# A clustered attention with an MLP: a step of the weights' narrowing on GpSimd, and other places for the first turned probabilities and the second queries

## The chip, the cores and the metric

One core of a Trainium2 chip (trn2) runs the whole program. Times are device microseconds. TensorE does the matmuls, VectorE, ScalarE and GpSimd the elementwise work, SyncE issues the DMAs.

## The reference

`q`, `k`, `v` have the shape (4, 8, 768, 64) in f32. Queries and keys are each given to one of 16 clusters of their head, and a query attends only to keys of its own cluster. The result, 3072 tokens x 512, goes through an MLP whose weights arrive in f64.

```python
q_assign = argmax(q_n @ c_n.T); k_assign = argmax(k_n @ c_n.T)       # normed
mask = q_assign[:, :, :, None] == k_assign[:, :, None, :]
scores = where(mask, scale * q @ k.T, -1e9)
attn = exp(scores - max); attn = attn / (sum(attn) + 1e-9)
x = (attn @ v), heads side by side                                    # 3072 x 512
h = x @ w_in                                                          # 512 x 2048
g = s * relu(h) ** 2 + b
out = g @ w_out                                                       # 2048 x 512
```

## The kernel before

**Units.** The attention is cut into 192 units: batch, chunk of 256 queries, pair of heads, half chunk, head. A unit is 128 queries against 768 keys. `scores` makes its 128x768 scores in PSUM from f16 halves, the cluster mask folded in; `maxima` takes the row maxima on VectorE (L533); `exps` has ScalarE make the bias (L540) and the probabilities `p` (L543), f32.

**The first 16 units** (`TURN`, `RAW`) turn `p` on TensorE (L567) into PSUM; VectorE and ScalarE copy one half each to `PT` (L142, L141), and `values` multiplies `PT` in f32 with the raw values (L591). From unit 16 on `p` is split into two f16 halves (`high`, `low`), turned by a DMA, and `value` multiplies them with the value halves `vh`, `vl` (L626 to L628). Those halves are made by `prep_v` (L491, L223, L225) in the tile `halves`, five places of one head pair each.

**Weights.** `weights` loads w_in and w_out in 32 pieces, 128x512 f64 each, as pairs of 32-bit words into stages: three buffers of the tag "stage", a part of `keys`, and `gs`. `rebase` (L246, ScalarE) turns the high word into an f32 whose exponent is moved, `narrow` (L250, L251, VectorE) shifts it up by three bits and puts the three top bits of the low word below. `bound` (L256 to L264) takes the sums and the maxima. Two pieces are asked for in every step of the main loop. A stage is loaded again (L92) once its piece is narrowed. When all are narrowed, `wsplit` (L309, L312) scales each piece and splits it into f16 halves.

**The MLP** follows 21 units behind (`LAG`): `mlp_in` (L684), `mlp_relu` (L691 to L694), `mlp_gl` (L699, GpSimd), `mlp_out` (L711), a step for each of 16 column blocks of each chunk. Its x tiles come from `finish_x` (L648, L651) into `xs_kept`, nine places. Until they are needed, three places at a time hold `kb` of the first batch's head pairs 1 to 3 (L353).

**Queries.** `prep_q` is a generator that the loop takes one yield further in each step: load, maximum over the chunk (L409, L412), scale (L415 to L418), split into `qb`, `qa` (L223, L225), copy (L429), DMA transposes into `QA`, `QB` (L433, L446), with the cluster mask between (L445). Chunk 0's two parts are made before the loop, chunk 1's begin at steps 6 and 14.

**Order.** The program is written once, unrolled, and a planner with its own times orders each engine's instructions by program order and readiness; units before 20 are asked for with priority (`first_of_all`), and some helpers are tied behind an instruction (`behind`). Each engine then takes its queue in order. Tiles of one tag share their places: `p`, `ph`, `PT`, `ka`, `qa`, `qb` and three of the first query loads have the tag "big", with 11 places (`BIGN`) of 3 KB a partition.

Of the kernel before, what the change touches and what calls it, by code (L numbers as in the profile page):

```python
# [8 lines left out]
F16 = mybir.dt.float16  # L9
BF16 = mybir.dt.bfloat16  # L10
F32 = mybir.dt.float32
I32 = mybir.dt.int32
U32 = mybir.dt.uint32
AF = mybir.ActivationFunctionType
ALU = mybir.AluOpType
# [3 lines left out]
P = 128  # L19
C = 16  # L20
D = 64
# [5 lines left out]
def tile_cluster_attention_mlp(ctx, tc, q, k, v, cent, w_in, w_out, s_in, b_in, out):  # L27
    nc = tc.nc
    B, H, S, _ = q.shape
    NT, DM = out.shape  # L30
    DFF = w_in.shape[1]
    T = S // P
    NP = H // 2
    CT = 2
# [5 lines left out]
    V = nc.vector  # L40
    G = nc.gpsimd
    A = nc.scalar
    LAG = 21
    BIGN = 11

    RAW = 16
# [5 lines left out]
    sb = ctx.enter_context(tc.tile_pool(name="sb", bufs=2))  # L52
# [5 lines left out]
    def const(shape, dt, name):  # L58
        return cp.tile(shape, dt, tag=name, name=name)
# [5 lines left out]
    def inverse2(eng, dst, src, e):  # L65
        eng.tensor_scalar(dst.bitcast(I32), src.bitcast(I32), -1, (254 + e) << 23, op0=ALU.mult, op1=ALU.add)

    def scale2(dst, src):
        bits = dst.bitcast(I32)
        V.tensor_scalar(bits, src.bitcast(I32), EXPMASK, None, op0=ALU.bitwise_and)  # L70
        V.tensor_scalar(bits, bits, -1, 253 << 23, op0=ALU.mult, op1=ALU.add)
        V.tensor_scalar(dst, dst, 2.0 ** 60, None, op0=ALU.min)
# [14 lines left out]
    def load(dst, src, free=False):  # L87
        if last_transpose[0] is None or free:
            nc.sync.dma_start(dst, src)
        else:  # L90
            with tc.issue_after(last_transpose[0].ins):
                nc.sync.dma_start(dst, src)  # L92
# [4 lines left out]
    def columns(n, name):  # L97
        return sb.tile([P, n], BF16, tag=f"amb{n}", name=f"amb_{name}", bufs=3)
# [10 lines left out]
    def allmax(dst, src, name, bank="m"):  # L109
        n = src.shape[1]  # L110
        if bank == "turned":
            pm = turned[:, 0]
        else:
            pm = small_bank(f"am_{name}", bank)
        for j in range(n):
            nc.tensor.matmul(pm[:, j * P : (j + 1) * P], src[:, j : j + 1].broadcast_to([P, P]), identb, start=True, stop=True)
        V.tensor_reduce(dst, pm[:, : n * P].rearrange("p (n q) -> p n q", q=P), axis=AX.X, op=ALU.max)

    def absmax(dst, src, axis=AX.X):
        return V.tensor_reduce(dst, src, axis=axis, op=ALU.max, apply_absolute_value=True)  # L120
# [69 lines left out]
    xs_kept = const([P, 9, CT, 2, P], F16, "xk")  # L190
# [4 lines left out]
    halves = const([P, 5, VHW + VLW], F16, "halves")  # L195
# [20 lines left out]
    def split(hi, lo, src, f, early):  # L216
        if early:
            A.activation(src, src, AF.Copy, scale=f)
            last_split[1] = A.activation(hi, src, AF.Copy)
            yield  # L220
            G.tensor_tensor(lo, src, hi, op=ALU.subtract)
        else:
            last_split[1] = A.activation(hi, src, AF.Copy, scale=f)  # L223
            yield
            last_split[0] = V.scalar_tensor_tensor(lo, src, f, hi, op0=ALU.mult, op1=ALU.subtract)  # L225
# [18 lines left out]
    def rebase(d):  # L244
        hw = d["st"][:, :, :, 1].bitcast(F32)
        A.activation(d["w"], hw, AF.Prelu, scale=2.0 ** -112, alpha=-(2.0 ** 32))  # L246

    def narrow(d):
        c = d["w"].bitcast(I32)
        V.tensor_scalar(c, c, 3, None, op0=ALU.logical_shift_left)  # L250
        V.scalar_tensor_tensor(c.bitcast(U32), d["st"][:, :, :, 0].bitcast(U32), 29, c.bitcast(U32),  # L251
                               op0=ALU.logical_shift_right, op1=ALU.bitwise_or)

    def bound(d):
        w, p, ft = d["w"], d["p"], d["ft"]
# [138 lines left out]
    def prep_q(b, c, hq):  # L394
        n = f"{b}_{c}_{hq}"
        nh = 4
        if b or c > 1 or c + hq > 1:
            qn = sb.tile([P, CT * DM], F32, tag="stage", name=f"qn_{n}", bufs=3)
        else:
            qn = sb.tile([P, T * P], F32, tag="big", name=f"qn_{n}", bufs=BIGN)  # L400
        qn = qn[:, : nh * CT * D].rearrange("p (h t d) -> p h t d", h=nh, t=CT)
        load(
            qn, q[b, nh * hq : nh * hq + nh].rearrange("h (p t) d -> p h t d", t=T)[:, :, c * CT : (c + 1) * CT, :]
        )
        yield
        prs = slice(2 * hq, 2 * hq + 2)
        sm = sb.tile([P, 4, 2], F32, tag="qsm", name=f"qsm_{n}", bufs=3)
        qm = columns(2, f"q{n}")
        absmax(qm, qn.rearrange("p (j h) t d -> p j (h t d)", j=2))  # L409
        if b + c:  # L410
            yield
        allmax(sm[:, 1, :], qm, f"q{n}", "m" if b or c > 1 else "h")  # L412
        yield
        f = sm[:, 2, :]
        scale2(f, sm[:, 1, :])  # L415
        V.tensor_tensor(f, f, KSM[b][:, 3, prs], op=ALU.min)
        V.tensor_tensor(sm[:, 1, :], f, KSM[b][:, 2, prs], op=ALU.mult)
        inverse2(V, sm[:, 3, :], sm[:, 1, :], -3)  # L418
        qa = sb.tile([P, 2 * T * P], F16, tag="big", name=f"qa_{n}", bufs=BIGN)[:, : nh * CT * 2 * D].rearrange("p (h t e d) -> p h t e d", h=nh, t=CT, e=2)
        qb = sb.tile([P, 2 * T * P], F16, tag="big", name=f"qb_{n}", bufs=BIGN)[:, : nh * CT * 2 * D].rearrange("p (h t e d) -> p h t e d", h=nh, t=CT, e=2)  # L420
        both = []
        for j in range(2):
            hs = slice(2 * j, 2 * j + 2)
            both.append(split(qb[:, hs, :, 0, :], qa[:, hs, :, 0, :], qn[:, hs], sm[:, 2, j : j + 1], b + c == 0))
        for z in zip(*both):
            yield
        for z in both:
            next(z, None)
        G.tensor_copy(qa[:, :, :, 1, :], qb[:, :, :, 0, :])  # L429
        QA = sb.tile([P, nh * CT, P], F16, tag="QA", name=f"QA_{n}", bufs=2)  # L430
        QB = sb.tile([P, nh * CT, P], F16, tag="QB", name=f"QB_{n}", bufs=2)
        QS[(b, c, hq)] = (QA, QB, sm)
        last_qa[0] = nc.sync.dma_start_transpose(QA, qa.rearrange("p h t e d -> p (h t e d)"))  # L433
        yield
        yield
        pa = small_bank(f"pq_{n}", "m" if b or c > 1 else "h")
        for h in range(nh):
            hc = slice((nh * hq + h) * C, (nh * hq + h + 1) * C)
            for t in range(CT):
                i = h * CT + t  # L440
                o = pa[:, i * C : (i + 1) * C]
                nc.tensor.matmul(o, QA[:, i, :], cT[:, 0, hc], start=True, stop=False)
                nc.tensor.matmul(o, QA[:, i, :], cT[:, 2, hc], start=False, stop=True)
        mk = qb.rearrange("p h t e (r c) -> p (h t) e r c", c=C)[:, :, 1, :, :]
        yield from onehot(pa, nh * CT, f"q{n}", mk, BIG, 0.0, G if b or c or hq else V)  # L445
        last_qb[0] = nc.sync.dma_start_transpose(QB, qb.rearrange("p h t e d -> p (h t e d)"))  # L446
# [108 lines left out]
    def low(i):  # L555
        u = U[i]
        if i < TURN:
            n = T // 2
            flat = sb.tile([P, T * P], F32, tag="big", name=f"PT_{i}", bufs=BIGN) if i < RAW else None
            two = None if i < RAW else sb.tile([P, 2, T * P], F16, tag="big", name=f"PT_{i}", bufs=BIGN)  # L560
            if i < RAW:
                u["PT"] = flat.rearrange("p (n q) -> p n q", n=T)
            else:
                u["PT"] = two.rearrange("p e (n q) -> p (e n) q", q=P)
            for e in range(2):
                for kt in range(n):
                    nc.tensor.transpose(turned[:, e, kt * P : (kt + 1) * P], u["p"][:, (e * n + kt) * P : (e * n + kt + 1) * P], ident)  # L567
                cols = slice(e * n * P, (e + 1) * n * P)
                if i < RAW:
                    done = copy((V, A)[e], flat[:, cols], turned[:, e, : n * P])  # L570
                    if i == RAW - 1:
                        last_copy[e] = done
                else:
                    A.activation(two[:, 0, cols], turned[:, e, : n * P], AF.Copy)
                    V.tensor_tensor(two[:, 1, cols], turned[:, e, : n * P], two[:, 0, cols], op=ALU.subtract)
            return
        G.tensor_tensor(u["ph"][:, 1, :], u["p"], u["ph"][:, 0, :], op=ALU.subtract)  # L577
        u["PT"] = sb.tile([P, 2 * T, P], F16, tag="big", name=f"PT_{i}", bufs=BIGN)
        last_transpose[0] = nc.sync.dma_start_transpose(u["PT"], u["ph"].rearrange("p e s -> p (e s)"))  # L579
# [229 lines left out]
    i = 0  # L809
    while i < NU + 8 or i - LAG < NS + 4:  # L810
# [28 lines left out]
        if 0 <= i - 1 < NU:  # L839
            with first_of_all(i):  # L840
                low(i - 1)
# [38 lines left out]
```

## Time and profile before

| | |
|---|---|
| median of 3 runs | 907.15 us (906.84 to 907.77) |
| profiled execution | 905.56 us, span 903.9 us |
| TensorE busy | 823.4 us (91%) |
| ScalarE busy | 710.7 us (79%) |
| VectorE busy | 636.9 us (70%) |
| GpSimd busy | 548.2 us (61%) |
| TensorE's mean granted clock | 0.971 |

Busy times are sums over the span, and instructions of one engine can overlap by some 0.1 us. The profile has views by stretch, by line, by tile, of waits, of the chain that ended last, and of the instructions in order of time. PE is TensorE, PEld its weight load, DVE VectorE, ACT ScalarE, POOL GpSimd, SPq SyncE's queue of DMAs. L12 is line 12 of the kernel.

### The profile page before, as it was taken

What the parts mean: (1) busy time and instruction counts of PE and PEld (TensorE: products, weight loads), DVE (VectorE), ACT (ScalarE), POOL (GpSimd) and SP (SyncE); (2) the same over time, 40 slices, a digit from 0 to 9 for tenths busy, and PEclk for the clock granted to TensorE, in tenths of its full rate; (3) what the DMA queues carried; (4) which work ended last, traced back from release to release, by engine and by line L of the source; (5) the groups of instructions that cost most, each with busy time, mean ns of one, the idle gap of its engine ahead of it and who ended that gap; (6) DMA issues with size and microseconds to landing.
All of it is one profiled execution on the core that took longest, in us unless ns stands there. A gap on an engine that the chain in (4) does not pass through costs nothing.

```text
span 903.9 us, 22830 instructions
## 1 busy us (share of the span) xinstructions
PE 823.4 (91%) x8625; PEld 584.7 (65%) x8625; DVE 636.9 (70%) x1673; ACT 710.7 (79%) x1406; POOL 548.2 (61%) x580
## 2 busy tenths in 40 slices
PE   1575869878999999999999999999999999999997
PEld 0464646545677767777766767777677777677764
DVE  8798898998778678658877667669777667563200
ACT  4578868875788879888888788987889888888553
POOL 3110147666587668768777677777876667576321
PEclk9996788997999999999999999999999999999999
DMA  5999536766797998979899879689997687676200
GB/s 154 214 334 305 158 71 147 163 138 137 159 184 151 193 199 144 180 146 187 173 168 205 192 150 181 165 142 198 188 158 166 129 138 162 121 157 122 59 25 23
DMA packets 437758, 144.23 MB, mean 160 GB/s; under 512 B 405392, under 2 KB 434064, under 8 KB 437648
## 3 DMA queue, kind: packets, MB, share of 16 engines
q1 hardware_dynamic: 437648, 142.78, 75.3%
q8 instruction: 67, 1.10, 0.6%
q14 instruction: 43, 0.35, 0.1%
HBM read 35.69 MB, written 6.29 MB: 46 GB/s over the span
## 4 chain that ended last, share of the span: by engine, by line
PE 51%; DVE 19%; DMA 12%; ACT 8%; issue 5%; POOL 2%; SPq 2%; DVEq 0%; ACTq 0%; POOLq 0%
PE h L684 18%; PE acc L711 16%; PE sc L523 8%; DVE ssm L533 3%; DMA kn<-in_k_dram 3%; DMA qn<-in_q_dram 2%; PE sc L626 2%; PE sc L628 2%; PE sc L627 2%; ACT p L543 2%; DVE ka L225 2%; DVE wis L312 1%; DMA vn<-in_v_dram 1%; ACT ssm L540 1%; SPq L579 1%
## 5 line engine op out<-in xcount | busy, mean ns | idle before, releaser
L577 POOL TENSOR_TENSOR ph<-p,ph 128x768 f16<-128x768 f32 x176 | 297.5, 1690 | 145.2 <-ACT ph L141 48.0
L684 PE MATMUL h<-xk,wis 128*128 128x256 f16 x2304 | 290.1, 276 | 10.6 <-DVE wis L312 3.3
L711 PE MATMUL acc<-wos,gs 128*128 128x512 f16 x1152 | 280.0, 379 | 2.2 <-DVE o L719 0.9
L684 PEld LDWEIGHTS <-wis 128*128 128x128 f16 x2304 | 223.6, 99 | 70.0 <-issue 4.1
L543 ACT ACTIVATE p<-sc,ssm,qsm 128x768 f32<-128x768 f32 x192 | 189.5, 987 | 4.1
L533 DVE TENSOR_REDUCE ssm<-sc 128x1 f32<-128x768 f32 x192 | 181.8, 948 | 3.2 <-PE sc L523 3.1
L699 POOL TENSOR_TENSOR gs<-r,gs 128x256 f16<-128x256 f32 x192 | 139.0, 725 | 67.2 <-ACT r L694 57.2
L711 PEld LDWEIGHTS <-gs 128*128 128x128 f16 x1152 | 104.0, 98 | 95.9 <-ACT gs L693 1.3
L540 ACT ACTIVATE ssm<-ssm,lift,qsm 128x1 f32<-128x1 f32 x192 | 73.5, 383 | 91.7 <-DVE ssm L533 91.3
L141 ACT ACTIVATE ph<-p 128x768 f16<-128x768 f32 x164 | 137.5, 838 | 0.5
L691 ACT ACTIVATE r<-h,cf 128x256 f32<-128x256 f32 x192 | 89.2, 465 | 37.6 <-PE h L684 30.8
L626 PE MATMUL sc<-halves,PT 128*128 128x65 f16 x1032 | 113.3, 196 | 0.3 <-DMA PT<-ph 0.3
L627 PE MATMUL sc<-halves,PT 128*128 128x64 f16 x1032 | 113.1, 193 | 0.0
L628 PE MATMUL sc<-halves,PT 128*128 128x65 f16 x1032 | 112.8, 193 | 0.0
L626 PEld LDWEIGHTS <-PT 128*128 128x128 f16 x1056 | 99.2, 98 | 12.1 <-DMA PT<-ph 0.9
L627 PEld LDWEIGHTS <-PT 128*128 128x128 f16 x1056 | 98.3, 99 | 11.7 <-issue 0.8
L523 PE MATMUL sc<-keys,QA 128*128 128x384 f16 x384 | 98.4, 338 | 7.9 <-ACT p L543 5.9
L523 PE MATMUL sc<-keys,QB 128*128 128x384 f16 x384 | 99.1, 339 | 6.0 <-DMA QB<-qb 5.9
L628 PEld LDWEIGHTS <-PT 128*128 128x128 f16 x1056 | 98.4, 98 | 0.0
L632 DVE TENSOR_SCALAR ssm<-sc 128x1 f32<-128x1 f32 x172 | 26.3, 153 | 82.4 <-PE sc L628 80.8
L694 ACT ACTIVATE r<-r 128x256 f32<-128x256 f32 x192 | 79.4, 415 | 3.8
L693 ACT ACTIVATE gs<-r 128x256 f16<-128x256 f32 x192 | 78.9, 412 | 1.3
(191 smaller groups left out, 1097.6 us busy)
## 6 DMA issues: line engine op xcount, KB each, us to landing
kn<-in_k_dram SPq DMA_DIRECT2D x16, 384.0 KB, 3.9
qn<-in_q_dram SPq DMA_DIRECT2D x24, 256.0 KB, 3.4
vn<-in_v_dram SPq DMA_DIRECT2D x16, 384.0 KB, 4.1
out_dram<-o SPq DMA_DIRECT2D x12, 512.0 KB, 3.4
wst<-in_moe_w_in_dram SPq DMA_DIRECT2D x10, 512.0 KB, 5.6
wst<-in_moe_w_out_dram SPq DMA_DIRECT2D x10, 512.0 KB, 5.7
PT<-ph SPq DMA_TRANSPOSE x176, 3.5
gs<-in_moe_w_out_dram SPq DMA_DIRECT2D x3, 512.0 KB, 4.4
```

The source lines that it names most:

```text
L141: return A.activation(dst, src, AF.Copy)
L523: last_score[0] = nc.tensor.matmul(sc[:, e, :HALF], X[:, col, :], y[:, h * S + e * HALF : h * S + (e + 1) * HALF], start=st, stop=not st)
L533: last_max[0] = V.tensor_reduce(SM[i // 4][:, 0, j : j + 1], U[i]["sc"], axis=AX.XY, op=ALU.max, negate=True)
L543: last_exp[0] = A.activation(p.rearrange("p (a b) -> p a b", a=2), u["sc"], AF.Exp, bias=bi, scale=u["scale"], **total)
L577: G.tensor_tensor(u["ph"][:, 1, :], u["p"], u["ph"][:, 0, :], op=ALU.subtract)
L626: nc.tensor.matmul(o1, PT[:, kt, :], vh[:, h, kt, : D + 1], start=(kt == 0), stop=False)
L627: nc.tensor.matmul(o, PT[:, kt, :], vl[:, h, kt, :], start=False, stop=False)
L628: nc.tensor.matmul(o1, PT[:, T + kt, :], vh[:, h, kt, : D + 1], start=False, stop=(kt == T - 1))
L684: nc.tensor.matmul(ph[:, :CW], WSP[ft][0][:, wl, kt, :], XS[(b, c, kt)][:, :, xl, :], start=(i == 0), stop=(i == len(terms) - 1))
L691: last_relu[0] = A.activation(r, ph[:, :CW], AF.Relu, scale=MS[(b, c)][0])
L699: G.tensor_tensor(g[:, 1, :], r, g[:, 0, :], op=ALU.subtract)
L711: nc.tensor.matmul(acc[:, t, :], g[:, gl, rows], WSP[ft][1][:, wl, :], start=(ft == 0 and gl + wl == 0), stop=(ft == NF - 1 and gl == 1))
```

## The change

Three edits. In `rebase` GpSimd turns the low word, in place in the stage, into its three top bits: as a number it is multiplied by 0.9375 / 2^29, 0.03125 is taken off, and the conversion to an integer gives 0 to 7. `narrow` is then one instruction, a shift by three and an or. In `prep_q` the tiles `qa`, `qb` of batch 0, chunk 1 (both parts) lie in places 4 to 7 of `xs_kept` and not in the tag "big". In `low` the turned probabilities of the first 16 units lie in places 0 to 3 of `halves`, by the unit's number modulo 4, and not in the tag "big".

```diff
     def rebase(d):
         hw = d["st"][:, :, :, 1].bitcast(F32)
         A.activation(d["w"], hw, AF.Prelu, scale=2.0 ** -112, alpha=-(2.0 ** 32))
+        lw = d["st"][:, :, :, 0]
+        G.tensor_scalar(lw, lw.bitcast(U32), 0.9375 * 2.0 ** -29, -0.03125, op0=ALU.mult, op1=ALU.add)
 
     def narrow(d):
         c = d["w"].bitcast(I32)
-        V.tensor_scalar(c, c, 3, None, op0=ALU.logical_shift_left)
-        V.scalar_tensor_tensor(c.bitcast(U32), d["st"][:, :, :, 0].bitcast(U32), 29, c.bitcast(U32),
-                               op0=ALU.logical_shift_right, op1=ALU.bitwise_or)
+        V.scalar_tensor_tensor(c.bitcast(U32), c.bitcast(U32), 3, d["st"][:, :, :, 0].bitcast(U32),
+                               op0=ALU.logical_shift_left, op1=ALU.bitwise_or)
...
-        qa = sb.tile([P, 2 * T * P], F16, tag="big", name=f"qa_{n}", bufs=BIGN)[:, : nh * CT * 2 * D].rearrange("p (h t e d) -> p h t e d", h=nh, t=CT, e=2)
-        qb = sb.tile([P, 2 * T * P], F16, tag="big", name=f"qb_{n}", bufs=BIGN)[:, : nh * CT * 2 * D].rearrange("p (h t e d) -> p h t e d", h=nh, t=CT, e=2)
+        if b == 0 and c == 1:
+            qa, qb = (xs_kept[:, j : j + 2].rearrange("p n t e q -> p (n t e q)") for j in (4, 6))
+        else:
+            qa, qb = (sb.tile([P, 2 * T * P], F16, tag="big", name=f"q{'ab'[j]}_{n}", bufs=BIGN) for j in range(2))
+        qa, qb = (z[:, : nh * CT * 2 * D].rearrange("p (h t e d) -> p h t e d", h=nh, t=CT, e=2) for z in (qa, qb))
...
-            flat = sb.tile([P, T * P], F32, tag="big", name=f"PT_{i}", bufs=BIGN) if i < RAW else None
+            flat = halves[:, i % 4, : 2 * T * P].bitcast(F32) if i < RAW else None
```

## Rows read from the trace of the kernel before

**Rows 1.** Busy us and instructions by stretch, granted clock, DMA share, GB/s.
```profile
25.00:110.00 85.00, 58.45 (x463) 46.45 (x463) 73.07 (x183) 64.72 (x144) 8.33 (x11) 0.84 0.92 257
110.00:130.00 20.00, 15.82 (x133) 11.83 (x132) 18.45 (x52) 15.61 (x28) 10.30 (x9) 0.91 0.25 54
130.00:220.00 90.00, 71.67 (x711) 48.24 (x712) 83.27 (x184) 66.16 (x127) 56.65 (x50) 0.89 0.62 141
220.00:400.00 180.00, 179.41 (x1980) 126.12 (x1978) 131.50 (x348) 150.13 (x291) 128.35 (x129) 1.00 0.90 174
```

**Rows 2.** SyncE's waits to 220 us: total, times, longest.
```profile
SPq L92 <- DVE wo L251: 12.0, 9, 2.1
...
SPq L92 <- DVE wi L251: 10.0, 7, 3.0
```

**Rows 3.** VectorE in order of time: start, us, line.
```profile
122.84 0.28 DVE L611 TENSOR_TENSOR xs<-px,ssm 128x128 f32<-128x128 f32 x1
```

**Rows 4.** The chain that ended last: start, us, what.
```profile
136.04 2.74 PE h L684 x12
```

**Rows 5.** The narrowing by line: busy us, mean ns of one.
```profile
L250 DVE TENSOR_SCALAR wi<-wi 128x512 int32<-128x512 int32 x15 | 6.3, 421 | 2.3 <-ACT wi L246 2.1
L250 DVE TENSOR_SCALAR wo<-wo 128x512 int32<-128x512 int32 x15 | 6.3, 418 | 1.2 <-ACT wo L246 1.2
L251 DVE SCALAR_TENSOR_TENSOR wi<-wst,wi 128x512 uint32<-128x512 uint32 x9 | 6.1, 682 | 0.0
```

**Rows 6.** GpSimd's groups by line, over the span.
```profile
L429 POOL COPY qa<-qb 128x512 f16<-128x512 f16 x24 | 17.9, 747 | 3.3 <-ACT qb L223 3.3
...
L337 POOL TENSOR_SCALAR qb<-oo_q 128x512 f16<-128x512 f16 x23 | 14.3, 624 | 15.4 <-DVE oo_q L336 8.2 <-DVE ssm L632 4.5 <-DVE ssm L633 1.2
...
L337 POOL TENSOR_SCALAR kb<-oo_k 128x768 f16<-128x768 f16 x12 | 10.0, 830 | 1.2 <-DVE oo_k L336 0.6 <-DMA qn<-in_q_dram 0.3 <-PE h L684 0.3
...
L376 POOL COPY xk<-ka 128x768 f16<-128x768 f16 x3 | 3.8, 1294 | 0.0
...
L142 POOL CAST ph<-p 128x768 f16<-128x768 f32 x3 | 2.5, 824 | 4.3 <-issue 4.3
```

**Rows 7.** One meeting of VectorE and GpSimd, in order of time.
```profile
88.47 1.17 DVE L251 SCALAR_TENSOR_TENSOR wi<-keys,wi 128x512 uint32<-128x512 uint32 x1
...
88.42 0.67 POOL L651 TENSOR_TENSOR xn<-xs,xn 128x256 f16<-128x256 f32 x1 [4.48 <-ACT xn L648]
```

**Rows 8.** Around the second queries, ScalarE and VectorE in order of time.
```profile
74.64 0.38 ACT L540 ACTIVATE ssm<-ssm,lift,qsm 128x1 f32<-128x1 f32 x1
...
90.47 0.49 ACT L223 ACTIVATE qb<-qn,qsm 128x256 f16<-128x256 f32 x1
90.86 0.97 ACT L543 ACTIVATE p<-sc,ssm,qsm 128x768 f32<-128x768 f32 x1
...
85.75 0.42 DVE L117 TENSOR_REDUCE qsm<-am_q 128x2 f32<-128x256 f32 x1
...
90.23 0.55 DVE L142 COPY PT<-turned 128x384 f32<-128x384 f32 x1
```

**Rows 9.** Busy by stretch, as in rows 1.
```profile
60.00:70.00 10.00, 6.47 (x59) 5.16 (x56) 10.00 (x26) 7.21 (x16) 2.44 (x3) 1.00 1.08 364
70.00:90.00 20.00, 11.33 (x68) 8.96 (x68) 17.68 (x49) 16.72 (x39) 1.49 (x2) 0.65 1.03 301
```

**Rows 10.** Around the value halves: instructions in time, and a tile's products.
```profile
113.77 0.78 PE L591 MATMUL px<-vn,PT 128*128 128x64 f32 x6
...
114.58 0.93 ACT L223 ACTIVATE halves<-vn,vm 128x768 f16<-128x768 f32 x1
...
L626 PE MATMUL sc<-halves,PT x120: 192/194/262, 126.3 to 228.1; 128*128 128x65 f16 x120
```

**Rows 11.** GpSimd's waits to 115 us: total, times, longest.
```profile
POOL xn L651 <- ACT xn L648: 23.0, 3, 14.9
POOL oe_k L334 <- DVE ssm L608: 21.9, 2, 19.6
```

## The prediction

> **What bounds the kernel now.** I read the busy times by stretch first. From 220 us on TensorE is busy 179.41 of 180 us to 400 [rows 1], and the slices of the page stay at nine tenths or more to the end: that part is TensorE's own work, and nothing in the change alters a matmul. The open time lies ahead of it: TensorE idles 26.6 us in 25 to 110, 4.2 in 110 to 130 and 18.3 in 130 to 220, 49 us in all. The engine that is full there is VectorE: 73.07 of 85, 18.45 of 20, 83.27 of 90 us (86%, 92%, 93%) [rows 1]. ScalarE has 64.72 of 85 and GpSimd only 8.33 of 85, so in the first stretch GpSimd is free for 76.7 us. The DMA engines show a share of 0.92 at 257 GB/s there.
>
> The first stretch is the loading of the 32 weight pieces (4 KB a partition). SyncE's waits show that the loads are held back by the narrowing: 12.0 and 10.0 us behind L251 [rows 2]. It closes where the first MLP step opens: the last xs product of the first x chunk comes at 122.84 [rows 3], the second step's matmuls of h run from 136.04 [rows 4]. Both inputs, weights and first 16 units, come through VectorE. What VectorE saves before 123 us therefore moves the whole TensorE-bound rest forward, until another resource is as full.
>
> **The change part by part.**
>
> *The shift that goes.* L250 is one instruction for each of 32 pieces, 15 + 15 of them at 421 and 418 ns in the rows, two more on pieces that lie in other tiles: 32 x 0.42 = 13.4 us of VectorE [rows 5], all while weights load. L251 stays one instruction with two SBUF operands of the same shapes; only its two operations change, and I keep its 682 ns.
>
> *The new GpSimd step.* 32 instructions of 128x512, one 32-bit operand with a step of two words, converted twice. No row shows this. Nearest below: the GpSimd scalar operation 128x512 in f16, 624 ns; in 128x768 32-bit words are no dearer than 16-bit ones (cast from f32 824, scalar operation in f16 830). Nearest above: the copies of 128x768 into xk at 1294 [rows 6]. I take 0.75, the mean of the 128x512 copies (747): 32 x 0.75 = 24 us, inside 76.7 us of idle GpSimd; at 1.29 it is 41 us and still fits. It runs beside ScalarE's L246 and waits for the same landing, so the narrowing starts when the later of the two is done. Queued behind it on GpSimd stand the first batch's cluster masks (L334, L337) and the xn differences (L651): each comes at most one step, 0.75 us, later.
>
> On the price, the Trainium skill (GPSIMD Engine Reference, section "Performance pitfalls for Q7 kernels") has a rule against this step: reads at a stride above 8 bytes cost about 2.9 cycles an element in place of 1.9. The step here is just 8 bytes, and no row here has it. By the page's 1.2 GHz the estimate would be 0.81 us on the near side and 1.24 on the far, and the gain summed up below would be smaller by 0.6 us, or by 5 us.
>
> *What it costs VectorE.* The two engines get in each other's way: L251 takes 0.68 us [rows 5], but 1.17 us at 88.47, when GpSimd's xn ran from 88.42 to 89.09 [rows 7]: 0.49 lost to an overlap of 0.62. With GpSimd's new step filling 24 of 85 us, 28% of the 32 L251 meet one, and lose half of 0.75: 32 x 0.28 x 0.375 = 3.4 us. Bounds: 0 (the planner sets them apart) and 32 x 0.49 = 15.7 (each meets one). Left on VectorE: 13.4 - 3.4 = 10.0 us. The row of VectorE's load says how much of that can be time: 86% of 10.0 = 8.6 us.
>
> *The places of the tag "big".* Probabilities p, their transposes PT, ka, qa and qb share 11 places. In the rows the exponentials wait for this tag: the bias of one unit was ready at 74.64 + 0.38, its scores stood in PSUM, ScalarE was working on weights, and yet its p came at 90.86. In the same half microsecond came the first write into qb (90.47) and into the next PT (90.23) [rows 8]. Three tiles of one tag starting together after 15 us says that the places are given out in program order and that qb, whose scale waits for the maximum L117 at 85.75, stood at the head. In the change neither qa, qb of these two chunks nor the 16 PT are asked of this tag, so p no longer queues behind them. What is that worth? VectorE was 89% busy in the gap, with weights [rows 9]: the exponentials move forward and weights back. Only the idle VectorE time can be won, 85 - 73.07 = 11.9 us in the stretch at most, nothing at least. I take 1 us, since the row for 70 to 90 has 2.3 us idle.
>
> *The new places' own waits.* PT of unit i lies where that of unit i-4 was, and needs values(i-4) done, one step earlier in program order: 0. The value halves of head pair 0 can now be written only after values(12). ScalarE writes them at 114.58 today; the last products of that call ran at 113.77 + 0.78 = 114.55 [rows 10], so nothing moves by more than it does already. If the planner were to put the two further apart, the first product that reads the halves is at 126.3 [rows 10], 10 us behind 114.58 + 0.93, with VectorE's half of the split between; ahead of that cover it costs nothing, beyond it every microsecond is one. The four memsets of the halves' last columns (L491), which wait for nothing today, now wait for values(12) and values(14) in GpSimd's queue, and the differences of p wait behind them: I charge 0.5 us, between 0 and 5. qa and qb of the two second chunks lie in kept tiles; the second pair comes eight steps after the first, and the key copies that lay there belong to steps up to 3: 0.
>
> **The sum.** 8.6 + 1.0 - 0.5 = 9.1 us. The profiled execution took 905.56 (span 903.9 and 1.66 around it), so 896.5; the median of the runs, 907.15, stands 1.59 above it, so 898.0.
>
> **The rivals.**
>
> *The loads pace it (0.15).* If the DMA's share of 0.92 is the limit, only the loop through a stage buffer shortens. 85 us for 32 pieces are 2.66 a piece, five stages make a loop of 13.3 us; 0.42 less in it is 3.2% of 85, 2.7 us: about 904.5. For it: the share. Against: 364 GB/s were reached in 60 to 70 beside 301 in 70 to 90 [rows 9], so the 21.8 MB of the stretch would need 60 us and not 85, and SyncE waited for L251.
>
> *Moving work between these two engines wins nothing (0.12).* At 1.29 us a step GpSimd fills 41 of 85 us, 48% of the L251 meet one and lose 0.65: 10 us of the 13.4, and 86% of 3.4 is 2.9, less the 0.5 of the places and with nothing from the gap, 2.4 at the best; and with each narrowing started late behind the longer step it is under the 1.8 us that can be told: 905.5 to 908. The Trainium skill (Perfetto Trace Analysis, section "Optimizing Scalar/DVE Operations") says as much: the two share a read port, so offloading from one to the other might not help. The trace agrees in kind (0.68 to 1.17 us); in size it has one such case in 32 pieces, since GpSimd is nearly idle.
>
> *Slower: the weights fall into GpSimd's queue (0.13).* GpSimd takes its instructions in order, and in this stretch it stands long behind others: 23.0 us in xn for ScalarE and 21.9 in oe_k for VectorE [rows 11]. Today that costs nothing. Put a weight step behind such a one and the narrowing waits, and VectorE behind it, and the next load. It decides from 9.1 us passed on, 20% of the 44.9; at a third it is 15 us, and the run ends at 907 + 6 = 913. Against: GpSimd issues of this kind are few (some 11 in 85 us), and the order written down follows when operands come.
>
> *More than that (0.13).* If the freed exponentials also close most of VectorE's 11.9 us of idle, the gain is near 10.0 + 6 = 16: 891.
>
> **How the numbers follow.** My forecast (893 to 902.5 is its own range) has 0.47. A measurement of this kernel tells 0.2%, 1.8 us, from no change. Faster: 0.47 + 0.13 + 0.15 = 0.75; same 0.12; slower 0.13. The range 888 to 909 leaves out about 0.04 below and 0.13 above; it holds the loads' rival, the rival without gain and the contention's and the gap's bounds but for their ends.
>
> **What would show it.** L250 gone and L251 still near 0.68 us, its mean under 0.8; a GpSimd group on the weight stages, 32 times, 0.6 to 0.9 us; the last narrowing some 7 us earlier; p within 2 us of its bias near unit 10; the second step's h 6 to 10 us before 136; TensorE's idle time to 220 near 41 us; the stretch behind it unchanged. I am wrong if VectorE shows waits for the GpSimd step beyond some 5 us, if that step takes over 1.3 us, if SyncE's waits for L251 vanish and the last load comes no earlier, or if value products wait for the halves.

## The result and the profile after

The changed kernel takes 917.23 us (median of 4 runs, 912.79 to 918.39) beside 907.0 of the kernel before (906.67 to 907.77): ratio 1.0103, 95% interval 1.0066 to 1.0139. By the ratio it is slower by about 9.3 us (10.2 between the two medians), where 9.1 us less was forecast. Its profiled execution took 916.1 us with a span of 914.4.

The lines of the changed kernel stand one lower from the weights on (narrowing L252, GpSimd's step L248), four lower from the scores on (p L547, h L688, relu L695, acc L715).

First the busy times by stretch, as in rows 1, and two stretches of the TensorE-bound part on their own.

```profile
25.00:110.00 85.00, 61.74 (x467) 49.45 (x468) 69.80 (x155) 66.28 (x147) 31.16 (x46) 0.83 0.93 260
110.00:130.00 20.00, 15.09 (x143) 12.21 (x143) 18.04 (x49) 15.45 (x27) 10.38 (x12) 0.86 0.32 67
130.00:220.00 90.00, 71.30 (x727) 47.80 (x727) 83.38 (x189) 66.09 (x127) 58.37 (x50) 0.92 0.68 140
220.00:400.00 180.00, 173.92 (x1909) 122.40 (x1906) 127.51 (x327) 148.19 (x286) 127.23 (x128) 1.00 0.86 168
...
325.00:420.00 95.00, 87.59 (x974) 62.67 (x973) 62.77 (x176) 76.35 (x152) 63.94 (x65) 1.00 0.82 154
420.00:560.00 140.00, 134.52 (x1527) 95.36 (x1525) 102.44 (x274) 115.11 (x224) 101.30 (x103) 1.00 0.86 173
```

The same two stretches in the kernel before:

```profile
325.00:420.00 95.00, 94.93 (x1072) 67.91 (x1070) 67.59 (x195) 83.23 (x163) 71.17 (x69) 1.00 0.89 166
420.00:560.00 140.00, 136.46 (x1535) 97.17 (x1534) 103.19 (x272) 116.20 (x228) 101.81 (x105) 1.00 0.89 177
```

From 25 to 220 us TensorE's work is about what it was: 148.1 us against 145.9 [rows 1]. The time is lost where nothing was edited. From 220 us to the end of the span, the changed kernel first, TensorE works as long as before and idles 22.7 us where it idled 10.9:

```profile
220.00:914.40 694.40, 671.73 (x7244) 475.00 (x7240) 443.73 (x1182) 554.59 (x1090) 463.04 (x470) 1.00 0.76 150
```
```profile
220.00:903.85 683.85, 672.94 (x7272) 475.51 (x7269) 441.23 (x1186) 554.14 (x1091) 461.92 (x470) 1.00 0.78 152
```

Most of that is one stretch: from 325 to 420 TensorE idled 0.07 us before and idles 7.41 now, at full clock in both. TensorE's waits from 220 to 620 us (what waited, for whom: us in total, times, longest), the changed kernel first, then the kernel before:

```profile
PE h L688 <- ACT r L695: 3.0, 2, 2.4
PE pk L389 <- DMA keys<-ka: 2.5, 1, 2.5
PE sc L527 <- ACT p L547: 2.2, 2, 1.3
PE am_q L116 <- DVE ssm L636: 1.9, 2, 1.1
PE acc L715 <- DVE o L723: 1.3, 1, 1.3
PE h L688 <- DMA xk<-xn: 1.1, 1, 1.1
```

```profile
PE sc L523 <- DMA QB<-qb: 1.9, 2, 1.3
PE acc L711 <- DVE o L719: 0.6, 1, 0.6
PE am_q L116 <- DVE ssm L632: 0.6, 1, 0.6
```

Many small waits of different kinds have come: for an MLP step's relu, for a key transpose of the third batch, for scores in PSUM whose probabilities are not yet made. Another order of the same instructions could look like that, and the programs bear it out: behind the first 44 units no instruction differs, yet 2070 of TensorE's 6947 from there on, 288 of VectorE's 1129 and 280 of ScalarE's 1043 stand in another place of their engine's queue. The planner has redone the rest from a slightly different start; why its new order is the worse one is not shown. Counted by relu instructions of the MLP, the changed kernel is 2.4 us ahead at the 41st, 4.4 behind at the 49th, 10.0 behind at the 97th and 10.5 at the last.

The edits themselves did what they say. The groups of GpSimd's step and of the narrowing to 110 us (busy us, mean ns of one | idle before):

```profile
L248 POOL TENSOR_SCALAR wst<-wst 128x512 int32<-128x512 uint32 x20 | 14.3, 717 | 25.3 <-DMA wst<-in_moe_w_in_dram 10.8 <-DVE ssm L609 6.0 <-DMA wst<-in_moe_w_out_dram 5.1
...
L252 DVE SCALAR_TENSOR_TENSOR wo<-wo,wst 128x512 uint32<-128x512 uint32 x9 | 7.0, 782 | 0.0
L252 DVE SCALAR_TENSOR_TENSOR wi<-wi,wst 128x512 uint32<-128x512 uint32 x9 | 6.6, 734 | 1.2 <-POOL wst L248 1.2
L252 DVE SCALAR_TENSOR_TENSOR wi<-wi,gs 128x512 uint32<-128x512 uint32 x3 | 3.0, 1002 | 0.0
...
L252 DVE SCALAR_TENSOR_TENSOR wo<-wo,gs 128x512 uint32<-128x512 uint32 x3 | 2.1, 688 | 1.1 <-POOL gs L248 1.1
```

And the eleventh unit's bias and probabilities, those of rows 8, on ScalarE; then the last narrowing, on VectorE, and the second MLP step's matmuls of h (start, us):

```profile
76.09 0.38 ACT L544 ACTIVATE ssm<-ssm,lift,qsm 128x1 f32<-128x1 f32 x1
...
78.34 0.97 ACT L547 ACTIVATE p<-sc,ssm,qsm 128x768 f32<-128x768 f32 x1
```

```profile
108.34 0.67 DVE L252 SCALAR_TENSOR_TENSOR halves<-halves,wst 128x512 uint32<-128x512 uint32 x1
```
```profile
132.89 2.74 PE L688 MATMUL h<-xk,wis 128*128 128x256 f16 x12 [1.89 <-DVE oe_q L333]
```

The wait of 16 us ahead of p [rows 8] is now 1.9. But the last weight is narrowed at 108.34, where it was at 103.85 before. The second step's h comes some 3 us ahead of the 136.04 of [rows 4].

### The profile page after: what moved, and what is told of

It reads as the page before. It is cut to its first block, busy times and chain, and to the rows that moved or that the text cites. A ratio compares the mean times of both kernels' runs of the same rounds, so it can differ in the third digit from the quotient of the medians.

```text
span 914.4 us, 22839 instructions
## 1 busy us (share of the span) xinstructions
PE 824.4 (90%) x8625; PEld 587.1 (64%) x8625; DVE 635.1 (69%) x1641; ACT 711.8 (78%) x1406; POOL 573.2 (63%) x612
## 5 line engine op out<-in xcount | busy, mean ns | idle before, releaser
L688 PE MATMUL h<-xk,wis 128*128 128x256 f16 x2304 | 289.1, 275 | 14.2 <-DVE oe_q L333 3.7
L715 PE MATMUL acc<-wos,gs 128*128 128x512 f16 x1152 | 285.3, 380 | 5.4 <-POOL gs L703 3.8
L688 PEld LDWEIGHTS <-wis 128*128 128x128 f16 x2304 | 223.8, 99 | 73.5 <-issue 10.1
L547 ACT ACTIVATE p<-sc,ssm,qsm 128x768 f32<-128x768 f32 x192 | 189.2, 985 | 4.0
L715 PEld LDWEIGHTS <-gs 128*128 128x128 f16 x1152 | 104.1, 98 | 96.5 <-POOL gs L703 5.2
L695 ACT ACTIVATE r<-h,cf 128x256 f32<-128x256 f32 x192 | 89.1, 465 | 46.3 <-PE h L688 37.7
```

Source lines behind the costliest of these rows:

```text
L547: last_exp[0] = A.activation(p.rearrange("p (a b) -> p a b", a=2), u["sc"], AF.Exp, bias=bi, scale=u["scale"], **total)
L688: nc.tensor.matmul(ph[:, :CW], WSP[ft][0][:, wl, kt, :], XS[(b, c, kt)][:, :, xl, :], start=(i == 0), stop=(i == len(terms) - 1))
L695: last_relu[0] = A.activation(r, ph[:, :CW], AF.Relu, scale=MS[(b, c)][0])
L715: nc.tensor.matmul(acc[:, t, :], g[:, gl, rows], WSP[ft][1][:, wl, :], start=(ft == 0 and gl + wl == 0), stop=(ft == NF - 1 and gl == 1))
```

## The experiments

Three theories. *Order*: the loss comes from the planner's new order of the untouched rest. *Edits*: one of the edits costs more than it saves. *Loads*: the saved VectorE time was worth less than I said, since the DMA engines pace the start too. To part them, kernels can hold each engine's queue to a recorded order by ties without semaphores between neighbours; the table of positions is left out here:

```diff
+    traced = nc.cur_bb.bb.instructions[cut:]      # cut: 0 (wholeorder) or where step 44 begins (oldtail, newtail)
+    for name, code in ORDER.items():              # per engine: the recorded order
...
+        for first, then in zip(line, line[1:]):
+            tc.add_manual_dep(then, first.name, DependencyInfo(NoSync, DATA), reason="order")
```

Each kernel was timed beside runs of the kernel before on the same chip (907.5 to 907.7 us in each set). One kernel's runs spread over 5 to 10 us, so the ratio with its interval is what counts. A difference worked out from two such ratios is less sure than either.

**The rest's order, both ways.** `changed_oldtail` is the whole change with the order of before from step 44 on; `before_newtail` is the kernel before with the changed kernel's order there.

> The changed kernel, all its work kept; what is traced from step 44 on (some 250 us into the run) is held, engine by engine, to the order that the kernel before has there. Theory 1 (the loss is the planner's new order of that part, whose instructions the change does not touch): the start's gain of 2 to 3 us stays and the loss of 13 us goes, 904 to 905.5 us. Rival (the new GpSimd step or the new places cost it, by what they do): as slow as the changed kernel, 913 to 918.

> The kernel before, none of the change; from step 44 on held to the changed kernel's order. Theory 1: the 13 us of loss appear without the change, 917 to 921 us. Rival: no edit, no loss, 906 to 908.

Measured: 907.86 us, ratio 1.0000 (0.9984 to 1.0017), and 915.16 us, 1.009 (1.0065 to 1.0115). Without any edit the new order alone costs some 8 us; without it the whole change costs nothing. Both sizes are under theory 1's forecast: the lead of 2 to 3 us that the start showed in the profile is not there in the time. TensorE's clock is no rival: its mean was 0.971 to 0.978 in the changed kernel's runs and 0.970 in those of the kernel before. The trace of `before_newtail` shows the same hole at the same place, and the same waits. The two stretches as above, then TensorE's waits from 220 to 620 us (its lines stand 31 lower than before's):

```profile
325.00:420.00 95.00, 87.63 (x973) 62.48 (x972) 63.93 (x176) 76.52 (x153) 64.11 (x64) 1.00 0.81 155
420.00:560.00 140.00, 135.38 (x1547) 96.11 (x1544) 102.99 (x277) 116.20 (x227) 101.50 (x104) 1.00 0.86 175
```

```profile
PE h L715 <- ACT r L722: 2.8, 2, 2.3
PE pk L419 <- DMA keys<-ka: 2.2, 1, 2.2
PE sc L554 <- ACT p L574: 1.7, 4, 0.8
```

**One edit at a time, the rest as before.** `bits_oldtail` has GpSimd's step and the shorter narrowing alone, `places_oldtail` both new places without them (the hunks of the change's diff that belong to each), each with the old order from step 44 on and the planner's own order ahead of it.

> Only the GpSimd step of the weights, the rest as before; from step 44 on in the order of the kernel before, so that the time shows the start alone. If the saved shift is worth what the prediction said, 898 to 900 (8.6 us). If the loads or the other queues take it back, 904 to 907. If GpSimd's queue delays the start, over 908.

> Only the new places (turned probabilities, second queries), the weights as before; from step 44 on in the order of the kernel before. If closing the gap before the eleventh exponential only swaps work on VectorE, 906 to 907 (the prediction gave it 1 us). If it is what gains the 2 to 3 us of the start, 904 to 905. Over 908 if the new places make waits of their own.

Measured: 903.55 us, 0.9956 (0.9934 to 0.9978), and 911.71 us, 1.0032 (1.0016 to 1.0047). The weights' step wins about 4 us, the places lose about 3, together nothing.

**Is the bad order tied to one edit?** `bits_ownorder` is the weights' step alone, with whatever order the planner gives.

```diff
-        V.tensor_scalar(c, c, 3, None, op0=ALU.logical_shift_left)
-        V.scalar_tensor_tensor(c.bitcast(U32), d["st"][:, :, :, 0].bitcast(U32), 29, c.bitcast(U32), ...)
+        V.scalar_tensor_tensor(c.bitcast(U32), c.bitcast(U32), 3, d["st"][:, :, :, 0].bitcast(U32), ...)
+        G.tensor_scalar(lw, lw.bitcast(U32), 0.9375 * 2.0 ** -29, -0.03125, op0=ALU.mult, op1=ALU.add)
```

> The kernel before with the GpSimd step and the shortened VectorE step alone, in the order that the planner itself gives (no order held). Theory 'order' (the ten us come from the way in which the planner reorders the untouched work from step 44 on; this kernel gets the same order there as the changed kernel but for some 200 places on TensorE's list): the 903.6 of the same edit with the order of before held there, plus 7.5 to 9.5: 911 to 913. Theory 'the places alone bring the bad order': 903 to 905.

Measured: 913.92 us, 1.0064 (1.004 to 1.0088). The best of the edits, alone, falls into nearly the same order (some 200 of TensorE's places differ from the changed kernel's) and loses 10 us by it.

**Why the weights' step is worth 4 us and not 8.6.** Five kernels in the order of before over the whole run, with only what is added to them placed freely. `bits_wholeorder` is the weights' step. The others take the kernel before and change one load: `noshift_wholeorder` leaves the shift out with no GpSimd step in its place (its weights then have other values), `extra_gpsimd_wholeorder` adds GpSimd's step and keeps both VectorE instructions, `two_shifts_wholeorder` shifts twice, and `more_dma_wholeorder` adds transfers that nothing waits for:

```diff
# noshift
-        V.tensor_scalar(c, c, 3, None, op0=ALU.logical_shift_left)
# extra_gpsimd
+        G.tensor_scalar(lw, lw.bitcast(U32), 0.9375 * 2.0 ** -29, -0.03125, ...)
# two_shifts
         V.tensor_scalar(c, c, 3, None, op0=ALU.logical_shift_left)
+        V.tensor_scalar(c, c, 0, None, op0=ALU.logical_shift_left)
# more_dma
         load(st.rearrange("p a f w -> p a (f w)"), src)
+        if p % 2 == 0:
+            nc.sync.dma_start(unread[p // 2], w_out.bitcast(I32)[ft * P : (ft + 1) * P, : 256])
```

> The same edit, with every engine's order of before held over the whole run (only the 32 GpSimd steps are placed freely). My prediction's step for the weights (8.6 us net) asks for 898 to 899. If what the planner did to the order of the start ate part of it: below 903. If the start is paced by something else than VectorE's saved shifts (loads, TensorE, GpSimd) and the order has no part in it: 903.6, as with the order of before from step 44 on alone. Over 905 if the planner's own new start was what earned the 4 us.

> The kernel before without the VectorE shift and without any GpSimd step, each engine's order of before held over the whole run. It leaves out the shift by three bits, so the weights' values are others; sizes and transfers stay. The GpSimd step with the shorter VectorE step gave 904 in this order, 4 us of the 13.4 us of VectorE time that went. If the DMA engines, which show a share of 1.0 and more from 35 to 100 us, pace the start, nothing more is to be had: 903 to 904.5. If GpSimd's 32 steps beside VectorE ate the rest: 898 to 900. If VectorE's 86% is the right price, as my prediction had it: 907.2 - 0.86 x 13.4 = 895.7, so 895 to 897.

> The kernel before with the 32 GpSimd steps added and VectorE's two instructions kept (the low three bits come out as zero), in the order of before. It measures by itself what the GpSimd steps cost through contention and through the wait that each narrowing gets. If the loads pace: 907 to 908.5. If contention eats half of the gain: 911 to 913. My prediction's 3.4 us at 86%: 910.

> The kernel before with a second shift (by zero) behind the first, 32 instructions of 0.42 us more on VectorE, in the order of before. If VectorE sets the pace at 86%: +11.5, so 918 to 920. If the loads pace and VectorE only has to keep up: its idle time from 35 to 100 us is some 6.5 us, so 13.4 us more push the start by some 5 to 7 us: 912 to 914.

> The kernel before with 16 extra transfers of 128 KB from DRAM to DRAM, one behind every second load of weights, which nothing waits for (2.1 MB beside the 21.9 MB of 25 to 110 us), in the order of before. If the DMA engines pace the start: 2.1 MB at 257 to 360 GB/s are 6 to 8 us: 913 to 915. If VectorE paces it and the transfers have room: 907 to 909.

| kernel | us | ratio to before (95%) | in us |
|---|---|---|---|
| `bits_wholeorder` | 904.59 | 0.9960 (0.9943 to 0.9977) | -3.6 |
| `noshift_wholeorder` | 905.73 | 0.9977 (0.9958 to 0.9997) | -2.1 |
| `extra_gpsimd_wholeorder` | 908.42 | 1.0024 (1.0001 to 1.0046) | +2.2 |
| `two_shifts_wholeorder` | 915.42 | 1.0089 (1.0058 to 1.0120) | +8.1 |
| `more_dma_wholeorder` | 911.71 | 1.0044 (1.0026 to 1.0063) | +4.0 |

The last column is 907.5 times the ratio less one. Taking 13.4 us off VectorE, even with nothing put on GpSimd, wins 2 to 4 us; putting 13.4 us on costs 8, between the two forecasts. So it isn't GpSimd's contention that ate the gain: without GpSimd's step no more is won in this order (905.73, over the 903 to 904.5 forecast for a start paced by the DMA engines). The stretch from 35 to 100 us shows what did not move, in the columns of rows 1: before, bits, noshift, two shifts, more DMA, in this order.

```profile
35.00:100.00 65.00, 46.07 (x351) 37.45 (x350) 58.51 (x144) 53.24 (x118) 6.88 (x9) 0.81 1.07 304
```
```profile
35.00:100.00 65.00, 47.41 (x347) 39.28 (x347) 50.62 (x115) 52.56 (x117) 28.29 (x39) 0.79 1.07 302
```
```profile
35.00:100.00 65.00, 47.17 (x349) 38.39 (x350) 49.87 (x115) 53.47 (x120) 6.40 (x9) 0.81 1.07 306
```
```profile
35.00:100.00 65.00, 43.30 (x322) 36.52 (x323) 60.27 (x153) 48.93 (x106) 7.37 (x9) 0.77 1.02 282
```
```profile
35.00:100.00 65.00, 45.72 (x341) 36.19 (x340) 56.03 (x136) 50.67 (x112) 6.87 (x9) 0.84 1.06 300
100.00:110.00 10.00, 6.24 (x60) 4.72 (x60) 9.55 (x26) 8.37 (x20) 0.83 (x1) 1.00 0.49 151
```

VectorE's busy time falls from 58.5 to 50 us, and the DMA engines' share stays at 1.07, their rate at 302 to 306 GB/s. With the extra transfers the rate does not rise either (300); the rest is pushed behind 100 us, where before only 38 GB/s moved. SyncE's waits for the narrowing show the same from the other side. First the weights' step alone, then two shifts, 25 to 110 us; before had 12.0 and 10.0 [rows 2]:

```profile
SPq L127 <- DVE wi L290: 7.7, 6, 2.6
SPq L431 <- POOL oe_q L373: 5.7, 1, 5.7
SPq L127 <- DVE wo L290: 5.5, 4, 2.0
```
```profile
SPq L128 <- DVE wo L291: 18.8, 10, 2.8
SPq L128 <- DVE wi L291: 11.1, 7, 2.9
```

8.8 us of these waits went, and the last piece was rebased no earlier: at 101.14 where it was at 100.28. With load added, VectorE sets the pace: the waits grow to 29.9 us and the DMA rate falls to 282 GB/s. With load taken away something else does; that it is the DMA engines' time fits the share and the rate, but is not shown. Two things speak for caution. The theory of the loads had asked 6 to 8 us for the extra transfers and got 4.0, and SyncE's waits for the narrowing stayed (12.1 and 9.8). And SyncE's queue did not get freer: all its waits from 25 to 110 us sum to 53.1 us before, to 58.8 with the weights' step and 53.7 without the shift. The loads share this queue, in a held order, with transposes that wait for a mask, and the waits for GpSimd rose from 11.8 to 22.2 and 18.9 us. No run parts the engines' time from this queue.

**The places, and the start's order.** Until here each kernel with the probabilities' places also had the planner's own start. `probs_oldtail` has these places alone; `bits_queries_oldtail` the weights' step with the queries' places; both keep the old order from step 44 on. The three `wholeorder` kernels hold the start too. Where the probabilities' places are in, the four memsets of the value halves are left free, since they must now wait for the products that read those places.

> The kernel before with the first turned probabilities in the value halves' places alone, from step 44 on in the order of before. The theory that these places cost the start (the exponentials come free earlier and push the weights later): 910 to 912, all of the 4 us that both places together cost. The rival, that the second queries' places among the kept x tiles cost it: 907 to 908 here.

> The GpSimd step and the second queries' places, without the probabilities' places, from step 44 on in the order of before. If the probabilities' places cost the 4 us: 903 to 904, as with the GpSimd step alone. If the second queries' places cost it: 907 to 908, as the whole change in the order of before.

> The first turned probabilities in the value halves' places alone, the four memsets placed freely, every other instruction in the order of before over the whole run. In the planner's own start it was 911.6. Theory 'the new start order costs': 907 to 908. Theory 'the places cost': 910 to 912.

> The GpSimd step and the second queries' places, every engine's order of before held over the whole run. With the planner's own start and the old order from step 44 on it was 901.5. If the two units of free room in the tag let the exponentials start earlier by themselves: 901 to 902. If the better start was the planner's order of it: 903.5 to 905, as with the GpSimd step alone in this order.

> The whole change, every engine's order of before held over the whole run, as far as the change allows it: the 32 GpSimd steps and the four memsets of the value halves' last columns are placed freely, since the new places forbid the old position of the memsets. If the planner's new order of the start costs what the new places seemed to cost (4 us): 902 to 904, as with the GpSimd step alone in this order. If the places cost it themselves: 907 to 908, as with the old order from step 44 on alone. My prediction's sum: 898.

| edits | planner's start, old order from step 44 | order of before throughout |
|---|---|---|
| weights' step | 0.9956 (0.9934 to 0.9978) | 0.9960 (0.9943 to 0.9977) |
| probabilities' places | 1.0037 (1.0023 to 1.0051) | 1.0018 (1.0002 to 1.0034) |
| weights' step, queries' places | 0.9938 (0.9914 to 0.9962) | 0.9981 (0.9959 to 1.0003) |
| all | 1.0000 (0.9984 to 1.0017) | 0.9984 (0.9965 to 1.0003) |

In us the medians of the right column stand at 904.59, 909.47, 907.06 and 906.21, of the left at 903.55, 911.58, 901.48 and 907.86. With the order held the probabilities' places still cost about 1.6 us, half of what they cost in the planner's start (the intervals overlap); my two theories for them expected 907 to 908 and 910 to 912, and the run fell between. So did the whole change, 906.21 between 902 to 904 and 907 to 908.

The trace shows a wait that they make: the last memset of the value halves stands in GpSimd's queue until products of the turned probabilities are done, and a cast of p stands behind it. First `probs_wholeorder`, then the kernel before:

```profile
123.35 0.12 POOL L529 MEMSET halves<- 128x24 f16 x1 [3.61 <-PE px L630]
123.41 0.82 POOL L178 CAST ph<-p 128x768 f16<-128x768 f32 x1
```
```profile
118.30 0.82 POOL L142 CAST ph<-p 128x768 f16<-128x768 f32 x1
```

The first product with the value halves then starts at 129.30 where it was at 126.25, and the second step's h at 138.10 where it was at 136.04. TensorE's granted clock from 118 to 124 us was also lower, 0.72 against 0.98, and this trace can't part the two.

What the queries' places are worth the held order can't show. It holds ScalarE to the order in which p stands behind the second queries' split, so the gap of rows 8 stays, whatever the places. The eleventh unit's bias and p, first in `bits_queries_wholeorder`, then in `bits_queries_oldtail`:

```profile
75.58 0.41 ACT L582 ACTIVATE ssm<-ssm,lift,qsm 128x1 f32<-128x1 f32 x1
...
91.66 0.97 ACT L585 ACTIVATE p<-sc,ssm,qsm 128x768 f32<-128x768 f32 x1
```
```profile
77.29 0.38 ACT L569 ACTIVATE ssm<-ssm,lift,qsm 128x1 f32<-128x1 f32 x1
...
79.08 0.97 ACT L572 ACTIVATE p<-sc,ssm,qsm 128x768 f32<-128x768 f32 x1
```

In the planner's own start both places together close the gap too (bias at 76.69, p at 78.10 in `places_oldtail`); the probabilities' places alone do not (77.34 and 94.03 in `probs_oldtail`), so it is the queries' that close it, and my theory that the probabilities' places cost time by freeing the exponentials is wrong. Both kernels with the queries' places missed their forecasts: 901.48 is under 903 to 904, 907.06 over 903.5 to 905. The version at 901.48, the weights' step with the queries' places and the old order from step 44 on, is the fastest here. It is clear of both kernels, but not of the weights' step alone (0.9938 and 0.9956, the intervals overlap). In its profiled run, the fastest of its seven, the last weight is narrowed at 100.68 and the first relu comes 10 us earlier than before (128.84 and 138.82); its runs also had more of TensorE's clock, 0.980 in the mean beside 0.970. How much of this is the closed gap and how much the rest of the planner's new start is open.

## Why the prediction was wrong

Predicted: 898.0 us, range 888 to 909. The sum of my steps beside what the runs showed, each from two ratios to the kernel before, times 907.5:

| step | predicted | measured |
|---|---|---|
| shift, GpSimd's step, contention | -8.6 | -3.6 |
| the tag "big" and the new places | -1.0 + 0.5 | +2.2 (0.9984 against 0.9960) |
| the planner's order of the start | none | +1.5 (1.0000 against 0.9984) |
| the planner's order from step 44 on | none | +9.3 (1.0103 against 1.0000) |
| all | -9.1 | +9.3 |

The first measured step and that from step 44 on are clear of their intervals; the two between are not, since the intervals of the ratios compared overlap. In the held order the gap stays, so the second row has what the places cost and not the 1.0 us that I gave to closing it.

*The step that failed most* is "TensorE's own work, and nothing in the change alters a matmul", and with it "the stretch behind it unchanged". Not one matmul changed, but their order did, and from 220 us on TensorE idled 11.8 us more for it. I read the planner only as the reason why freed work would be put well, never as something that redoes the untouched rest. No rival held it either; the slower one was GpSimd's queue, and at 913 it lay near the result by accident: VectorE waited 2.3 us for GpSimd's step, far from its 9.1.

*The price of saved VectorE time.* The instructions went as counted, and VectorE's busy time from 35 to 100 us fell by 7.9 us in the held order. But not 86% of the saving was time, only 3.6 of the 10.0 us. The rival of the loads had the size, though its cause is not shown: 904.5 forecast, 904.59 measured in that order (903.9 by the ratio). I held against it that 364 GB/s had been reached, so that 60 of the 85 us would do for the bytes. That took a rate for a limit. The first two lines below, neighbours in the kernel before, have a share above 1 at 398 and at 188 GB/s; in the first 76 of 1266 packets are under 512 B, in the second, while a key transpose is under way, 1573 of 1983. So as high a share can come with half the rate. Nor is the share a plain limit: it reaches 1.34 elsewhere (third line). It counts the packets' time, and since packets overlap it can pass 1 though the engines rest: in the second stretch nine of 40 slices are all but empty (last line, busy tenths by slice). The share of 0.92 that I took for 25 to 110 us was 1.07 from 35 to 100 us, with 0.71 ahead of it and 0.16 behind.

```profile
50.00:55.00 5.00, 5.00 (x50) 4.68 (x50) 4.47 (x11) 4.51 (x11) 0.46 (x1) 0.80 1.06 398
55.00:60.00 5.00, 3.95 (x52) 3.34 (x51) 5.00 (x13) 4.91 (x11) 0.09 (x1) 1.00 1.21 188
...
485.00:490.00 5.00, 5.00 (x49) 3.47 (x48) 3.27 (x7) 4.46 (x11) 4.38 (x4) 1.00 1.34 199
```
```profile
DMA  8998999944239999999999600010100029499999
```

And it was my own mark: wrong "if SyncE's waits for L251 vanish and the last load comes no earlier". In the changed kernel these waits fall from 22.0 to 6.5 us, and the last narrowing comes 4.5 us later. In the held order 8.8 us of them vanished, and the last piece came no earlier.

*GpSimd's step.* Right. Its mean is 0.71 us (22.8 us for 32), where I took 0.75, and most are at 0.65. My estimates from the Trainium skill's cycles per element on the two sides of its rule on strides (GPSIMD Engine Reference, section "Performance pitfalls for Q7 kernels") were 0.81 and 1.24; the measurement lies under both, and decides. (The 0.6 us less of gain that I gave for 0.81 is 0.5 by my own sum.)

*Contention.* Right in size. The 32 narrowings take 24.7 us to 110 us where 32 at 0.682 [rows 5] would be 21.8: 2.9 lost, 3.4 forecast; beside the 22.5 us that they took in all in the kernel before, it is 2.2. By itself, `extra_gpsimd_wholeorder`, it costs 2.2 us of the run (0.1 to 4.2).

*The gap.* Right that p would no longer queue behind the second queries: it comes 1.9 us after its bias and not 16, and the queries' places do it. The reason was half right: the gap also stays with both new places in when ScalarE keeps the order of before (bias at 74.75, p at 90.88 in `changed_wholeorder`), so the places act through the planner's order. Whether it is time stays open. In the held order of `bits_wholeorder` the gap stays and 3.6 us are won; in the changed kernel it closes, and weights take the place that the exponentials left: the last narrowing is 4.5 us later, where the prediction asked for 7 us earlier. In `bits_queries_oldtail` it closes, and the last narrowing is 3.2 us earlier.

*The new places' own waits.* The wait that I named, value halves' memsets in GpSimd's queue with the differences of p behind them, is there: the cast of p comes 5.1 us later in the held order. I charged 0.5 us, with 5 as the far end. The probabilities' places alone cost 1.6 us (0.2 to 3.1) in that order.

## What to carry to other kernels

Where a list scheduler lays out a long unrolled program, an edit at the start can re-order all that follows, and here that alone was worth 8 to 10 us, more than each of the edits; so compare an edit with the order of the untouched rest held, before judging it, and keep the better order afterwards. But a held order also holds what the edit would have let move: it shows what an edit costs, not what freedom it gives. Where a resource is nearly full and others stand close behind it, the price can be asymmetric: here 13.4 us off VectorE won 2 to 4, the same on top cost 8. Read a DMA share with its stretch cut where the transfers end, and don't take the highest rate seen for its limit.

## What had not been expected of the hardware

The DMA engines' share was as high at 188 GB/s (1.21), with mostly small packets, as at 398 (1.06). GpSimd took 0.65 us for 128x512 words at a step of two words, read as unsigned numbers and written as integers, a few hundredths more than its f16 scalar operation on as many elements (0.624 [rows 6]).
